# Linear attention with exponential features, then a gated causal layer: operand transposes of half the units by the DMA crossbar, feature weights by fp32 transfers, another order of products, and a new list

## The chip, the cores and the metric

The kernel runs on one core of a Trainium2 chip. The metric is the device time of one execution in microseconds (us), the median of several runs. A core has a tensor engine (PE; its weight loads are listed apart as PEld), a vector engine (DVE), a scalar engine (ACT), GpSimd (POOL) and a sync engine (SP). Each of them works through its own instructions in order, and semaphores make one wait for another. Products land in PSUM, which has 8 banks of 128 partitions by 512 fp32 numbers. Transfers run on 16 DMA engines. They are issued here from SP, ACT and POOL, and a transfer that changes the type is issued from POOL.

## The reference

For each of 8 batches and 8 heads, 576 tokens of 64 numbers are projected to 128 features, shifted by their largest magnitude, and taken through `exp` with both signs. The head outputs, side by side, then go through a gate and two matrix products.

```python
def phi(x):                                     # x: [8, 8, 576, 64], w_phi: [64, 128]
    proj = einsum('bhsd,df->bhsf', x, w_phi)
    proj = proj - max(abs(proj), axis=-1, keepdims=True)
    return concatenate([exp(proj), exp(-proj)], axis=-1)
q_p, k_p = phi(q), phi(k)
kv  = einsum('bhsf,bhsd->bhfd', k_p, v)
z   = sum(k_p, axis=2)
attn = einsum('bhsf,bhfd->bhsd', q_p, kv) / (einsum('bhsf,bhf->bhs', q_p, z)[..., None] + 1e-6)
x = attn.transpose(0, 2, 1, 3).reshape(8, 576, 512)
gate_pre[t] = sum over k of conv_w[k] * x[t + k - 4]       # causal, 5 taps
out = (sigmoid(gate_pre) * (x @ w_val)) @ w_out
```

## The kernel before

A *unit* is one pair of heads of one batch, its first 512 tokens: units 0 to 31, four to a batch. Units 32 to 39 are *tails*: the last 64 tokens of all heads of one batch. Each unit passes through small operations, and one string, `ORDER`, lists all of them by hand for the whole kernel, as `name.unit@banks:engine`. An engine's instructions stand in the order in which the list names them; semaphores are put in where one operation needs another. So the list alone sets what each engine, SP's and POOL's queues among them, does next, and a step that waits holds up all that stands behind it on its engine.

The operations of a unit, by their names in the list, with the line numbers of the old program:

- `LD` issues the loads of K, Q or V of a batch from POOL, fp32 in DRAM to bf16 in SBUF (L171, L177). Three batches of each have room.
- `T` transposes the unit's K and Q for the projection: eight 128x128 transposes on PE into one bank (L387). `C` copies the bank to SBUF, on DVE or ACT (L241, L239). The pool of these tiles `T` has room for five units.
- `PK`, `PA`, `PQ` are the projections by the feature weights `W2`: K with tokens on the partitions, Q likewise (for its largest magnitudes alone), and Q with features on the partitions (L437, L645). With `:W` they go over all 128 rows of the array with zero-padded weights (`W2Z`).
- `MA`, `MB`, `MQ` take the largest magnitudes on DVE (L503, L488). For units 0 and 1, and for tails, `MQ` writes `MQA`, and `SA`, which subtracts the maxima from `PQ`'s banks on PE, takes them straight from there (L661). For the others `MQ` writes `MQX`, `MT` transposes that on PE (L554), `MC` copies the result to `MQT`, and `SA` multiplies from `MQT`.
- `KA`, `KB` take the exponentials of K, one bank each, with both signs (L532). `XA`, `XB` take those of Q, one bank each, with both signs (L545): four instructions of 512 columns. Tails use `X0`, `X1`: one sign each, over both banks (L570).
- `E` and `V` scale V and its column of ones by the exponential of the maxima, mostly on POOL (L563, L609). `KV` sums K features times V over 16 matmuls of 65 columns and two of the tail (L622, L627); `KM` copies the result. `N` multiplies by the Q features, 16 matmuls of 65 columns (L699); `XN` divides on DVE (L717, L719). `XP` transposes the quotient into `XT`: by the DMA crossbar from SP for units 0 to 27 (L738), on PE for the last four and for tails, with `XX` copying the bank.

Per batch follow the gate (`GF`, `GT` on PE, `TH`, `HT` on ACT), the value product (`VA`, `VB`, L805), its product with the gate (`GV` on DVE, L821), the output product (`OA`, `OB`, L834), its copy (`OE`, on ACT L843 or DVE L845) and the stores from SP (`ST`, `SU`; at the end `SL`, half of whose transfers ACT issues). `HL` copies the first columns of `XT`, on POOL. `FL` multiplies zeros: matmuls that only keep PE running.

At the start, K of the first unit comes as fp32 by one transfer from SP and one from ACT, Q likewise behind it, and ACT and DVE cast them (`CK`, `CQ`). The feature weights come by one transfer from POOL that casts and repeats them, into `W2` (L195), from which `WB` fills `W2Z` on DVE.

## Time and profile before

| | |
|---|---|
| median of 3 runs | 231.88 us (231.78 to 236.46) |
| the profiled execution's own time | 231.9 us |
| its span (first to last instruction) | 230.1 us |
| mean granted TensorE clock | 0.985 of full speed |
| moved by DMA | 31.35 MB, mean 136 GB/s |

The page gives, for one profiled execution, each engine's busy time as a share of the span. A row of a group names line, engine, operation, `out<-in` with the shapes, the count, the busy time and the mean duration of one instruction, and the idle time just before them. Busy time is the union of the intervals, so that instructions that overlap count once. The chain that ended last is followed back from the last instruction: at each step to what released it, or to the instruction before it on its engine. A row of the timeline gives the start, the duration, the engine (ACTq and SPq are the queues that issue transfers) and what ran.

### The profile page before, as it was taken

The numbers are of one execution on the slowest core, as the hardware profiler recorded it, in microseconds if no ns is written. First come the engines' busy times: TensorE is split into PE (matmuls) and PEld (weight loads), VectorE is DVE, ScalarE is ACT, GpSimd is POOL, SyncE is SP. The second block draws the span as 40 slices with busy tenths as digits, with TensorE's granted clock in tenths as the row PEclk, the third lists the DMA queues.
The fourth block names the chain that finished last, engine by engine and source line by source line (L and its number), as shares of the span: only waits on it lengthen the run. The fifth ranks groups of instructions, "written<-read, shape, count | busy, mean of one in ns | idle before, by whom it ended". The sixth has DMA issues, their size and how long they took to land.

```text
span 230.1 us, 8985 instructions
## 1 busy us (share of the span) xinstructions
PE 204.2 (89%) x3834; PEld 140.6 (61%) x3862; DVE 190.2 (83%) x347; ACT 190.7 (83%) x419; POOL 130.9 (57%) x168
## 2 busy tenths in 40 slices
PE   0675989877989999999998999899999999999996
PEld 0363678556747576566756765668567666566642
DVE  6579999968889999879995999979998998757351
ACT  3189899996799999989998999899997989585530
POOL 8976668699299719393487343590299019500100
PEclk9999799999899999999999999999999999999999
DMA  6999974699969938899557796179940928403746
GB/s 123 190 203 219 262 131 51 99 239 126 150 91 198 191 78 117 132 191 193 87 71 129 99 161 179 50 105 145 227 117 6 140 46 187 115 3 95 177 140 187
DMA packets 42242, 31.35 MB, mean 136 GB/s; under 512 B 17877, under 2 KB 38229, under 8 KB 42202
## 3 DMA queue, kind: packets, MB, share of 16 engines
q0 software_dynamic: 21856, 14.93, 45.8%
q1 hardware_dynamic: 19802, 15.01, 30.7%
q10 hardware_dynamic: 544, 0.84, 1.2%
q8 instruction: 30, 0.49, 0.9%
q14 instruction: 10, 0.08, 0.1%
HBM read 32.58 MB, written 9.44 MB: 183 GB/s over the span
## 4 chain that ended last, share of the span: by engine, by line
PE 54%; ACT 27%; DVE 11%; issue 3%; DMA 3%; POOL 1%; DVEq 0%; ACTq 0%; POOLq 0%
ACT KT L532 10%; ACT QT L545 10%; PE PS L834 9%; PE PS L805 9%; PE PS L622 5%; PE PS L699 5%; PE PS L437 5%; DVE MQX L488 4%; PE PS L387 3%; PE PS L778 3%; PE PS L645 3%; DMA W<-in_w_phi_dram 3%; PE PS L661 2%; PE PS L282 2%; PE PS L885 2%
## 5 line engine op out<-in xcount | busy, mean ns | idle before, releaser
L609 POOL TENSOR_TENSOR VT<-vN,EA 128x1024 bf16<-128x1024 bf16 x30 | 57.2, 1905 | 43.1 <-ACT EA L563 30.1
L532 ACT ACTIVATE KT<-PS 128x512 bf16<-128x512 f32 x128 | 69.0, 660 | 8.3 <-DVE MKA L503 6.1
L545 ACT ACTIVATE QT<-PS 128x512 bf16<-128x512 f32 x128 | 68.8, 649 | 5.4 <-PE PS L661 5.2
L503 DVE TENSOR_REDUCE MKA<-PS 128x4 f32<-128x512 f32 x64 | 42.9, 682 | 2.4 <-PE PS L437 2.2
L488 DVE TENSOR_REDUCE MQX<-PS 128x8 bf16<-128x1024 f32 x30 | 36.6, 1219 | 3.4 <-PE PS L437 3.2
L805 PE MATMUL PS<-XT,WVAL 128*128 128x512 bf16 x128 | 35.4, 380 | 0.2
L834 PE MATMUL PS<-WOUT,GV 128*128 128x512 bf16 x108 | 31.3, 380 | 1.6 <-issue 1.1
L437 PE MATMUL PS<-W,T 64*128 64x128 bf16 x488 | 25.2, 226 | 2.8 <-ACT QT L545 0.8
L821 DVE SCALAR_TENSOR_TENSOR GV<-GATE,PS 128x512 bf16<-128x512 bf16 x32 | 21.4, 681 | 4.0 <-PE PS L805 3.8
L241 POOL COPY XT<-XT 128x1008 bf16<-128x1008 bf16 x8 | 8.2, 1031 | 27.8 <-DVE XT L241 19.8
L437 PEld LDWEIGHTS <-T 64*128 64x128 bf16 x488 | 16.7, 97 | 11.6 <-issue 7.1
L719 DVE TENSOR_TENSOR XN<-PS,RCPA 128x512 bf16<-128x512 f32 x32 | 22.1, 692 | 1.1
L622 PE MATMUL PS<-VT,KT 128*128 128x65 bf16 x512 | 22.1, 196 | 1.0 <-POOL VT L613 0.5
L241 DVE COPY T<-PS 128x1024 bf16<-128x1024 bf16 (+1 forms) x31 | 20.4, 666 | 2.3 <-PE PS L387 2.2
L699 PEld LDWEIGHTS <-QT 128*128 128x128 bf16 x512 | 19.6, 100 | 4.0 <-issue 0.6
L622 PEld LDWEIGHTS <-KT 128*128 128x128 bf16 x512 | 19.7, 99 | 3.7 <-issue 0.6
L699 PE MATMUL PS<-KVSA,QT 128*128 128x65 bf16 x512 | 21.4, 196 | 0.4 <-ACT KVSA L239 0.2
L600 POOL TENSOR_TENSOR VTZ<-vN,EA 64x512 bf16<-64x512 bf16 x16 | 16.7, 1042 | 8.7 <-ACT EA L563 8.2
L387 PE MATMUL PS<-ident_bf,kN 128*128 128x128 bf16 x128 | 13.6, 234 | 5.8 <-ACT kN L239 5.5
L794 ACT ACTIVATE GATE<-PS 128x1024 bf16<-128x1024 f32 x16 | 15.7, 1020 | 3.4 <-PE PS L778 3.4
L387 PE MATMUL PS<-ident_bf,qN 128*128 128x128 bf16 x128 | 13.7, 234 | 3.2 <-DVE qN L241 2.1
L834 PEld LDWEIGHTS <-GV 128*128 128x128 bf16 x128 | 10.4, 97 | 8.9 <-issue 1.2
(104 smaller groups left out, 367.6 us busy)
## 6 DMA issues: line engine op xcount, KB each, us to landing
out_dram<-OS SPq DMA_DIRECT2D x28, 256.0 KB, 3.9
kN<-in_k_dram POOLq DMA_DIRECT2D x14, 320.0 KB, 6.6
vN<-in_v_dram POOLq DMA_DIRECT2D x14, 320.0 KB, 7.2
qN<-in_q_dram POOLq DMA_DIRECT2D x7, 576.0 KB, 7.8
OS<-in_moe_w_val_dram SPq DMA_DIRECT2D x1, 1024.0 KB, 9.1
out_dram<-OSt SPq DMA_DIRECT2D x8, 128.0 KB, 2.4
vN<-in_v_dram POOLq DMA_DIRECT2D x4, 160.0 KB, 8.3
OS<-in_moe_w_out_dram SPq DMA_DIRECT2D x2, 256.0 KB, 6.7
```

The lines of the kernel that those rows point to most:

```text
L241: read(engines[eng].tensor_copy(dst, x), bank)
L387: nc.tensor.transpose(u.Tps[:, x, blk, :], a, ident_bf[:, :])
L437: nc.tensor.matmul(PS[:, bank[par], c0 + blk * P:c0 + (blk + 1) * P], u.T[r, i, blk, :], W2[r, :], start=True, stop=True,)
L488: read(nc.vector.tensor_reduce(MQX[:, i // G % NG, :].rearrange("p (r c) -> p r c", r=2)[:, :, c:c + 4], tokview(u.PA, 0, u, None), AX.X, ...
L503: read(nc.vector.tensor_reduce(out, half_ps(bank, x, out, wide), AX.X, ALU.max, apply_absolute_value=True,), [bank[x]])
L532: read(nc.scalar.activation(out, half_ps(u.PK, x, out, u.PKwide), AF.Exp, scale=1.0 if ft == 0 else -1.0,), [u.PK[x]])
L545: read(nc.scalar.activation(dst, PS[:, u.PQ[x], :].rearrange("p (x t) -> p x t", t=64), AF.Exp, scale=1.0 if ft == 0 else -1.0,), [u.PQ[x]])
L609: e.tensor_tensor(u.VT[:, :, :, 0:D], x.unsqueeze(1).to_broadcast([P, 2, n, D]), w.unsqueeze(3).to_broadcast([P, 2, n, D]), ALU.mult,)
L622: nc.tensor.matmul(PS[:, bank[0], c:c + E1], u.KT[:, ft, j // 2, j % 2, :], u.VT[:, ft, j, :], start=(ft == 0 and j == 0), stop=False, ski ...
L699: nc.tensor.matmul(PS[:, bank[c // 2], x * E1:(x + 1) * E1], u.QT[:, ft, c, h2, :, :].rearrange("p j t -> p (j t)"), kv[:, ft, h2, :], sta ...
L805: nc.tensor.matmul(PS[:, m.val[jt], :], WVAL[:, dt, jt * P:(jt + 1) * P], planes(xt(m.b), slice(0, P), dt, 4), start=(dt == 0), stop=(dt = ...
L834: nc.tensor.matmul(PS[:, bank, :], lhs(jt), WOUT[:, jt, :], start=(jt == 0), stop=(jt == 3))
```

## The change

1. K and Q of units 16 to 31 are no longer transposed by `T` and copied by `C`. Two transfers from SP for each unit, `TK` and `TQ`, write the tile `T` through the DMA crossbar. The function was in the program before, but the list didn't call it.
2. The feature weights come as fp32, by one transfer from SP and one from ACT between K and Q of the first unit. ACT casts them to `W2` (`W`), and DVE casts them to `W2Z` (`WB`). POOL's transfer is gone.
3. Units 2 to 7 take the way of units 0 and 1: `MQ` writes `MQA`, and `MT` and `MC` fall away (`MTF = 8`).
4. `KV` and `N` issue the same products in another order: four consecutive ones go to four places of the bank instead of adding to one place. `N` now has one start flag for each bank.
5. The list is new. Besides other banks and places, all units use `X0`, `X1` in place of `XA`, `XB`; the first K is cast by DVE; a clearing of `VTZ` (`VZ`), three of the four `DF` copies and three `HL` copies go from POOL to DVE; four units' `V` run on DVE instead of two; 16 projections have `:W` instead of 10; 7 `FL` stand within the kernel and 17 at its end, instead of 9 and 15.

```diff
+MTF = 8
 ORDER = """
-LD.1 CK.0:A LC.0 WB.0:D LD.0 CQ.0:D T.0@4 C.0:D LD.2 FL.6@6 LD.3 TX.0@0 CX.0:D PK.0@7,6 T.1@0 MA.0 C.1:D KA.0
+LD.1 CK.0:D W.0:A VZ.0:D T.0@1 C.0:D FL.16@0 FL.6@4 CQ.0:D WB.0:D PK.0@2,7 MA.0 TX.0@3 CX.0:D MB.0 LD.0 T.1@4
...
     main_dma((nc.sync, nc.scalar), "k", 0, 0, 1, first["k"])
+    W2 = const.tile([P, F], BF16, name="W2")
+    wtmp = const.tile([P, F], FP32, name="wtmp")
+    for t in range(2):
+        (nc.sync, nc.scalar)[t].dma_start(wtmp[t * 64:(t + 1) * 64, :], w_phi[:, :])
...
-    W2 = const.tile([P, F], BF16, name="W2")
-    nc.gpsimd.dma_start(W2[:, :], w_phi.unsqueeze(0).to_broadcast([2, D, F]))
...
+    def op_W(i, eng):
+        copy(eng, W2[:, :], wtmp[:, :])
+
     def op_WB(i, eng):
         for x in range(2):
             r = slice(x * 64, x * 64 + 64)
-            copy(eng, W2Z[r, x, :], W2[r, :])
+            copy(eng, W2Z[r, x, :], wtmp[r, :])
...
-        elif i < 2:
+        elif i < MTF:
             bankmax(MQA[:, i, :, :], u.PA, 0, u, u.PAwide)
...
     def op_KV(i, bank):
-        for ft in range(2):
-            for j in range(8):
-                c = (2 * ft + j // 4) * E1
+        for jj in range(4):
+            for x in range(4):
+                ft, j = x // 2, x % 2 * 4 + jj
+                c = x * E1
                 nc.tensor.matmul(
                     PS[:, bank[0], c:c + E1], u.KT[:, ft, j // 2, j % 2, :], u.VT[:, ft, j, :],
-                    start=(ft == 0 and j == 0), stop=False, skip_group_check=True,
+                    start=(jj == 0 and x == 0), stop=False, skip_group_check=True,
                 )
...
     def op_SA(i):
-                if u.tail or i < 2:
+                if u.tail or i < MTF:
...
     def op_N(i, bank):
-        for c in range(4):
-            for h2 in range(2):
-                x = (c % 2) * 2 + h2
-                for ft in range(2):
+        for half in range(2):
+            for ft in range(2):
+                for x in range(4):
+                    c, h2 = 2 * half + x // 2, x % 2
                     nc.tensor.matmul(
-                        PS[:, bank[c // 2], x * E1:(x + 1) * E1],
+                        PS[:, bank[half], x * E1:(x + 1) * E1],
                         u.QT[:, ft, c, h2, :, :].rearrange("p j t -> p (j t)"),
                         kv[:, ft, h2, :],
-                        start=(ft == 0), stop=(ft == 1),
+                        start=(ft == 0 and x == 0), stop=(ft == 1), skip_group_check=True,
                     )
```

The function behind `TK` and `TQ`, and that behind `X0` and `X1` (both unchanged):

```python
    def crossbar(i, x, name):
        u = units[i]
        if not hasattr(u, "T"):
            u.T = ktp.tile([P, 2, 4, P], BF16, name="T")
        j = 0 if name == "q" else 1
        nc.sync.dma_start_transpose(
            u.T[:, x, :, :], main[name, u.b][:, u.hp, j:j + 8, :].rearrange("p j d -> p (j d)"),
        )

    def qexp(u, ft):
        ...
        exps(u.QT[:, ft, :, :, :, :].rearrange("p c h r t -> p r (c h) t"), u.PQ, 4, ft)
```

Three places show how instructions move. A row gives the line, the operation and `out<-in` with the shape (x2: twice in a row); the new program's lines stand some six further down. The first is DVE behind the clearings that open the kernel. Before:

```order
L241 COPY W2Z<-W_111 64x128 x2
L241 CAST qN<-GV 128x576
L241 COPY T<-PS 128x512 x2
L503 TENSOR_REDUCE MKA<-PS 128x4
L241 COPY T<-PS 128x1024
```

Now:

```order
L243 CAST kN<-GV 128x640
L270 MEMSET VTZ_141 128x1040
L243 COPY T<-PS 128x512
L243 CAST qN<-GV 128x576
L243 CAST W2Z<-wtmp 64x128 x2
L508 TENSOR_REDUCE MKA<-PS 128x4
```

The cast of K and the clearing of `VTZ` have come to DVE, the copy of the first transposed K stands ahead of the cast of Q, and `W2Z`, on which nothing of the first unit rests now, stands behind both. The first maximum of K (`MKA`) stands right behind these.

The second place is SP, from the last crossbar transposes of batch 1 on. `XT<-XN` are the quotients (`XP`), `T<-qN` and `T<-kN` the new transfers, `out_dram` the stores. Before:

```order
L738 DMA_TRANSPOSE XT1_130<-XN_1269 128x4x128
L738 DMA_TRANSPOSE XT1_130<-XN_1369 128x4x128
L738 DMA_TRANSPOSE XT0_128<-XN_1804 128x4x128
L855 DMA out_0_dram<-OS_1722 64x1024 x2
L738 DMA_TRANSPOSE XT0_128<-XN_1888 128x4x128
L738 DMA_TRANSPOSE XT0_128<-XN_1946 128x4x128
```

Now:

```order
L744 DMA_TRANSPOSE XT1_132<-XN_1360 128x4x128
L402 DMA_TRANSPOSE T_1857<-qN_1415 128x4x128
L744 DMA_TRANSPOSE XT0_130<-XN_1869 128x4x128
L744 DMA_TRANSPOSE XT0_130<-XN_1826 128x4x128
L402 DMA_TRANSPOSE T_1968<-qN_1415 128x4x128
L744 DMA_TRANSPOSE XT0_130<-XN_1921 128x4x128
L744 DMA_TRANSPOSE XT0_130<-XN_1991 128x4x128
L402 DMA_TRANSPOSE T_1968<-kN_1425 128x4x128
L402 DMA_TRANSPOSE T_2275<-kN_1425 128x4x128
L402 DMA_TRANSPOSE T_1857<-kN_1425 128x4x128
L402 DMA_TRANSPOSE T_2275<-qN_1415 128x4x128
```

The transfers of K and Q of batch 4 (units 16 to 18 here) stand among and behind the four quotients of batch 2. SP has 60 crossbar transposes in all where it had 28.

The third place is ACT at the end of the kernel: `GATE` are the last gates, `OS` and `OSt` the copies of output products, the DMA rows the stores that ACT issues itself. Before:

```order
L794 ACTIVATE GATE0_5182<-PS_97 128x1024
L794 ACTIVATE GATE1_5203<-PS_97 128x1024
L843 ACTIVATE OSt_5221<-PS_97 128x512
L843 ACTIVATE OS_5232<-PS_97 128x512
L855 DMA out_0_dram<-OS_5232 64x512
```

Now:

```order
L800 ACTIVATE GATE0_4961<-PS_97 128x1024
L800 ACTIVATE GATE1_4975<-PS_97 128x1024
L900 ACTIVATE GATEt_5004<-PS_97 128x256
L849 ACTIVATE OS_5014<-PS_97 128x512
L861 DMA out_0_dram<-OS_5014 64x512
```

Before, one more copy and the other stores follow on ACT, while DVE copies two of the last four products; the tail's product `OSt` was copied ahead of them. Now the pair of copy and store stands four times on ACT, one behind the other, and the copy of the tail's product comes behind all of them as ACT's last instruction.

More of the change, by code (lines that the diff above doesn't have):

```diff
@@ L107 @@
+XX.39:D XX.28:A OE.27:A XP.31@5 OE.23:A ST.11 XX.31:D HL.7:D OB.26 OE.26:A VA.28@6 VA.30@7 GF.7@4,5,0,1 TH.14
+VA.31@3 VB.28 VA.29@2 GV.28 ST.13 VB.31 TH.15 VB.29 GV.29 VB.30 GV.31 GV.30 GT.7@4,5 HT.7 OA.30@0 OA.31@6
+OA.29@1 OB.30 OE.30:A OB.31 SL.30 OE.31:A SL.31 VT.7 GW.7 OB.29 OE.29:A SL.29 OA.28@0 OB.28 OT.3@6 OE.28:A
+SL.28 FL.15@2 FL.19@7 FL.20@0 FL.10@2 FL.11@5 FL.21@3 FL.4@2 FL.12@1 FL.5@7 FL.22@0 FL.23@0 FL.13@7 FL.8@5
+FL.0@0 FL.3@0 OF.3:A FL.14@0 SU.3 FL.2@0
 """
```

146 lines of the change are left out of this document (70 added, 76 removed).

## The prediction

> **What bounds the kernel now.** I read the page's busy times first, then the busy times in windows of 10 us, the chain that ended last with its shares and its pieces, and last the groups and the timeline where the change touches them. The page:
>
> ```profile
> span 230.1 us, 8985 instructions
> PE 204.2 (89%) x3834; PEld 140.6 (61%) x3862; DVE 190.2 (83%) x347; ACT 190.7 (83%) x419; POOL 130.9 (57%) x168
> ```
>
> Three engines stand within 6% of each other, so no single one bounds the whole. The windows say which does where (columns: stretch, its length, then each engine's busy time and count, granted PE clock, DMA share, GB/s):
>
> ```profile
> 20.00:30.00 10.00, 7.62 (x114) 5.11 (x113) 9.40 (x16) 8.91 (x22) 5.84 (x10) 0.83 1.26 247
> ...
> 110.00:120.00 10.00, 9.67 (x147) 6.31 (x143) 9.83 (x19) 10.00 (x25) 7.14 (x9) 1.00 0.46 65
> ...
> 180.00:190.00 10.00, 9.85 (x179) 6.94 (x180) 9.82 (x20) 9.41 (x24) 1.04 (x1) 1.00 0.55 92
> ```
>
> Where units 16 to 31 run, PE and DVE are at 97 to 99%, and ACT at 94 to 100%. POOL and the transfers have room. The chain, by share of the span, and in a second answer by share of the 94 us from 96 to 190 us alone, agrees:
>
> ```profile
> by line: ACT KT L532 10.2%; ACT QT L545 9.6%; PE PS L834 9.3%; PE PS L805 9.2%; PE PS L622 5.2%; PE PS L699 4.9%; PE PS L437 4.8%; DVE MQX L488 3.8%; PE PS L387 3.4%; PE PS L778 3.4%; issue 3.1%; PE PS L645 2.7%; DMA W<-in_w_phi_dram 2.5%;
> by line: ACT KT L532 13.5%; PE PS L805 9.5%; ACT QT L545 9.2%; PE PS L834 7.6%; PE PS L622 7.0%; PE PS L437 6.0%; PE PS L699 5.6%; PE PS L778 5.6%; PE PS L387 3.4%; PE PS L645 3.4%; DVE MQX L488 2.6%; issue 2.5%; PE PS L661 2.2%; ACT QTt L5
> ```
>
> It changes between PE and ACT all the time, with DVE in between. A cut on one engine alone would soon meet the next; this change takes work from all three.
>
> **Part 1: crossbar for K and Q of units 16 to 31.** What PE spends on these transposes, and DVE on their copies, over all 32 units:
>
> ```profile
> L387 PE MATMUL PS<-ident_bf,qN 128*128 128x128 bf16 x128 | 13.7, 234 | 3.2 <-DVE qN L241 2.1 <-issue 1.1
> L387 PE MATMUL PS<-ident_bf,kN 128*128 128x128 bf16 x128 | 13.6, 234 | 5.8 <-ACT kN L239 5.5 <-issue 0.2
> L241 DVE COPY T<-PS 128x1024 bf16<-128x1024 bf16 x29 | 19.6, 684 | 1.9 <-PE PS L387 1.9
> ```
>
> Half of 27.3 us of PE goes: 13.7 us. Of the copies, DVE loses 17 at 0.68 us, 11.5 us. On the chain they weigh less. From 96 to 190 us L387 has 3.4% of 94 us, 3.2 us. Three copies stand there as well, with other rows used below:
>
> ```profile
> 27.32 3.90 ACT QT L545 x8
> ...
> 112.50 0.92 ACT T L239
> ...
> 148.90 0.69 DVE T L241
> ...
> 161.65 0.92 ACT T L239
> ...
> 204.80 0.52 PE PS L622 x16
> 205.86 0.49 PE PS L699 x16
> ```
>
> They make 2.5 us, so 5.7 us of the chain go. I take that, since the chain shows what the end rests on; the bounds are 0 (the next engine is as late) and 13.7 us. What is late next is ACT, at 10.00 of 10 us in the window from 110 us.
>
> The new work lies on SP and the DMA engines: 32 transfers, each like a quotient's:
>
> ```profile
> L738 SPq DMA_TRANSPOSE XT<-XN x28: 1188/1197/2072, 34.7 to 189.1; - x28
> DMA to landing us min/median/max: 2.4/3.4/4.6
> q1 hardware_dynamic: 1632, 0.39, 19.3%
> ```
>
> Issuing takes 32 x 1.2 = 38 us of SP, which then has 60 x 1.2 = 72 us of transposes in 230. The last row is from 180 to 190 us, where four transposes alone ran on that queue: 19.3% of 10 us is 0.48 us of all 16 engines for each, 15 us for 32, or 7% of the span. I price both at nothing. The cover is the distance in the list: `TQ.17` and `TQ.16` stand some two units ahead of their projections, `TK.16` a whole gate ahead, and 3.4 us of landing fit into less than a unit (200 us / 32 = 6 us). Behind each on SP stand quotients and stores. A store can wait; a quotient held up holds the gate. If the cover fails, this is rival C.
>
> **Part 2: feature weights and opening.** The order of DVE and ACT at the start, before:
>
> ```profile
> 3.77 0.93 DVE L226 MEMSET VTZ<- 128x1040 bf16 x1 [0.17 <-issue]
> 4.69 0.27 DVE L230 MEMSET MQX<- 128x256 uint32 x1
> 7.32 0.58 DVE L241 COPY W2Z<-W 64x128 bf16<-64x128 bf16 x2 [2.36 <-DMA W<-in_w_phi_dram]
> 7.94 0.67 DVE L241 CAST qN<-GV 128x576 bf16<-128x576 f32 x1
> 8.53 0.41 DVE L241 COPY T<-PS 128x512 bf16<-128x512 bf16 x1
> 4.72 0.74 ACT L239 ACTIVATE kN<-GV 128x640 bf16<-128x640 f32 x1 [1.09 <-DMA GV<-in_k_dram]
> 10.57 2.06 ACT L532 ACTIVATE KT<-PS 128x512 bf16<-128x512 f32 x4 [5.11 <-DVE MKA L503]
> GV<-in_q_dram ACTq DMA_DIRECT2D x1, 144.0 KB, 4.2
> GV<-in_q_dram SPq DMA_DIRECT2D x1, 144.0 KB, 5.0
> ```
>
> DVE waits 2.36 us for the weights, and the first copy of `T` stands behind that wait. Now DVE, free at 4.96 us, casts K (0.74 us, ACT's price), clears `VTZ` (0.93), copies `T` (0.41, done at 7.05), casts Q (0.67) and `W2Z` (0.58). It reaches the first maximum at 8.3 us, and that takes 0.7 us: the first exponential at about 9.0 us instead of 10.57, so 1.5 us less. The weights take the place in the queues that Q had (4.2 to 5.0 us to landing, issued near 1.5 us), so they land by 6.5 us, ahead of the copy. Bounds: 0 if they come 1.5 us later, 2.5 us if POOL's earlier loads help as well (its weight transfer and its clearing are gone).
>
> **Part 3: exponentials of Q in two instead of four.** ACT's rows:
>
> ```profile
> L545 ACT ACTIVATE QT<-PS 128x512 bf16<-128x512 f32 x128 | 68.8, 649 | 5.4 <-PE PS L661 5.2
> L794 ACT ACTIVATE GATE<-PS 128x1024 bf16<-128x1024 f32 x16 | 15.7, 1020 | 3.4 <-PE PS L778 3.4
> 217.38 1.94 ACT L794 ACTIVATE GATE<-PS 128x1024 bf16<-128x1024 f32 x2 [0.85 <-PE PS L778]
> ```
>
> Back to back, 512 columns cost 3.90 / 8 = 0.49 us (row above) and 1024 columns 1.94 - 1.02 = 0.92 us. A unit gains 4 x 0.49 - 2 x 0.92 = 0.12 us, 32 units 3.8 us of ACT. On the chain L545 has 9.6% of 230 us, 22 us of 32 x 1.96 = 63 us, a third; so I take 1.2 us, with bounds of 0 and 6.1 us (by the busy shares, 68.8 / 128 = 0.54 and 15.7 / 16 = 0.98 us). The Trainium skill, page "ScalarE: Activation LUTs", section "What ACT_TABLE_LOAD costs", gives an ACTIVATE 186 ns and 0.833 ns per column, of which 93 ns overlap with the next: by that the pair of 512 and 1024 columns would be 0.52 and 0.95 us, 6.0 us over all units, and this term 2.0 us instead of 1.2. The trace's 0.49 us is nearer to the columns alone than the page has it.
>
> **Part 4: order of products.** `KV` ran 16 products in 0.52 us, `N` the same size in 0.49, where only pairs add to one place. If four places make `KV` as quick, its chain share (5.2% of 230 = 12 us) falls by 6%, 0.7 us. Bounds 0 and 2 us. `N` gains nothing.
>
> **Part 5: units 2 to 7 without `MT` and `MC`, more wide projections, moves to DVE.** Priced at nothing: in the first third ACT hides what PE and DVE do more, since PE had 2.4 us of 10 free in the window from 20 us. Two more `V` on DVE cost about the 3.9 us that its copies leave four times over. Bounds 1 us of gain (a shorter way from maximum to exponential) and 2.5 us of loss.
>
> **Part 6: the end.** ACT's last rows, and the chain's:
>
> ```profile
> 223.43 0.51 ACTq L855 DMA_DIRECT2D out_dram<-OS  x1
> 223.99 0.60 ACT L843 ACTIVATE OS<-PS 128x512 f32<-128x512 f32 x1 [0.59 <-PE PS L834]
> 224.61 2.03 ACTq L855 DMA_DIRECT2D out_dram<-OS  x3
> ...
> 220.61 4.26 PE PS L834 x19
> ```
>
> Four pairs of copy (0.60) and issue (0.51), and then the tail's copy, make 5.0 us on ACT, from the first product's end on. Before, DVE had two of the copies, and ACT two copies and four issues. PE has 12 output products behind the first (4.26 / 19 = 0.22 us each) and a tail's value product, some 3 us. So the end lies about 1 us further behind the last product than before; bounds 0 and 1.5 us. The 17 `FL` behind it cost nothing beside the stores' landing.
>
> **Sum.** -1.5 (opening) - 5.7 (crossbar) - 1.2 (exponentials) - 0.7 (products) + 0 + 1.0 (end) = -8.1 us: a span of 222.0 us. The profiled execution took 231.9 us with a span of 230.1, so 1.8 us lie around it, and it equals the median of 231.88. That gives 223.8 us.
>
> **The rivals.**
>
> A, *all three engines get lighter and the chain shortens with them*: PE's busy time falls by its full 13.7 us and nothing else comes late. Then the sum is -16.1, and the time 215.8 us. For it speaks that PE and DVE are both near 10 of 10 in the window from 180 us; against it that ACT loses only some 4 of 190.7 us.
>
> B, *ACT is the bound*, as in the window from 110 us. PE's and DVE's relief turns into idle time. What is left is the opening (1.5), the exponentials' full 3.8 us at most, and 1.8 us of ACT's copies of `T`, less 1.0 at the end: at most 6.1 us, and 3.5 us with the chain's share of the exponentials. The time is 226 to 228.4 us, within 2%. Against it: PE has the larger share of the chain.
>
> C, *SP's order holds the projections up*, the case on the slower side. A `TK` waits for K's load and for a free `T` tile, and all behind it waits too, quotients included. Were each of 16 units to wait 0.5 us, the 8.1 us would be gone; from 0.8 us each (8.1 + 4.6 = 12.7 us) it is slower by 2%. With the slowest landing, 4.6 us, instead of 3.4, a unit whose transfer is just in time loses 1.2 us, and the time is 223.8 + 19.2 = 243 us. Against it: the transfers stand a unit or more ahead.
>
> D, *PE pauses long enough to be clocked down*. In the window from 20 us PE was busy for 7.62 of 10 us and had 0.83 of its clock; at 9.67 it had all. If the missing transposes open such pauses in three windows, PE loses 17% of 10 us in each, 5 us: 228.8 us. The Trainium skill, page "TensorE: Matmul & The Clock Gate", section "Part 1: The HAM clock gate (the "warmup" mystery)", says that the clock halves after an idle window of some 3.4 us; the row at 0.83 fits that in kind, but no row after 110 us does.
>
> E, *the order of products does nothing*: 224.5 us, inside the forecast.
>
> **How the numbers follow.** The forecast, with E in it (221 to 226 us), gets 0.53, A (215 to 221) 0.22, B (226 to 229) 0.14, D 0.04 and C 0.07. About 2% is what a measurement of this kernel tells from no change: 227.2 and 236.5 us. Faster takes the forecast, A and 0.04 of B: 0.79. Within 2% lie the rest of B, D and a mild C: 0.16. Slower is the rest of C: 0.05. The range goes from A's 215.8 to B's 228.8 us and leaves out the best of A and C, some 0.15.
>
> **What would show it.** In the changed profile the first `KT` exponential should start near 9.0 us; L387 should have half its count; a pair of `QT` rows should show 0.92 us to the next; `KV` should show 0.49 us for 16; PE should never wait for `T<-kN` or `T<-qN`; ACT's busy share should rise. A wait of `PK` or `PQ` for a DMA row of 0.5 us or more in each unit, or ACT at 95% and more, would make the prediction wrong.

## The result, and the profile after

The changed kernel took 244.29 us (median of 4 runs, 242.92 to 246.21), where the kernel before took 231.78, 231.88, 236.46 and 238.62 us in the same comparison (median 234.17). Some executions of a kernel are 1.5% or more slower than its fastest, and the medians here and below take them in while the ratios leave them out, so the ratio is the one to go by where the two differ. The ratio is 1.054, with a 95% interval of 1.042 to 1.067: slower by 5% or 12.5 us, where 223.8 us and a range of 215.8 to 228.8 us were forecast. The profiled execution took 246.21 us, its span is 244.4 us, and the mean granted clock of PE fell from 0.985 to 0.951.

The page of the changed kernel gives the busy times and the chain by engine:

```profile
span 244.4 us, 8652 instructions
PE 205.2 (84%) x3693; PEld 137.1 (56%) x3720; DVE 192.5 (79%) x340; ACT 186.6 (76%) x353; POOL 122.5 (50%) x155
PE 36%; DVE 26%; ACT 16%; DMA 15%; issue 3%; POOL 2%; ACTq 1%; DVEq 0%; SPq 0%; POOLq 0%
```

The three engines have about the busy time that they had before, in a span that is 14.3 us longer. So none of them became the bound; they wait together. The chain shows for what: transfers have 15% of it, some 37 us (before, they had 3%). PE's busy time should have fallen by a dozen us, and it rose by one. The groups show a part of the reason (count, then busy us and mean ns):

```profile
L392 PE MATMUL PS<-ident_bf,kN 128*128 128x128 bf16 x64 | 7.5, 247 | 7.2 <-DVE kN L243 5.4 <-issue 1.3 <-ACT QTt L575 0.3
L392 PE MATMUL PS<-ident_bf,qN 128*128 128x128 bf16 x64 | 7.4, 248 | 1.0 <-DVE qN L243 1.0
...
L811 PE MATMUL PS<-XT,WVAL 128*128 128x512 bf16 x128 | 34.8, 397 | 0.0
```

The transposes are down to 14.9 us from 27.3. But the same 128 value products, which had 380 ns each, now have 397. Over the whole kernel the mean clock, 0.951 instead of 0.985, stretches 205 us of work on PE by some 7 us (an estimate from these numbers); the rest of the dozen isn't accounted for. The windows (columns as before the change: PE, PEld, DVE, ACT, POOL, clock, DMA share, GB/s) show where PE slowed down:

```profile
40.00:50.00 10.00, 6.05 (x76) 4.23 (x71) 9.10 (x15) 5.94 (x10) 9.65 (x12) 0.71 0.41 79
70.00:80.00 10.00, 6.62 (x151) 4.54 (x145) 4.99 (x9) 4.79 (x9) 5.38 (x8) 0.75 0.99 136
110.00:120.00 10.00, 9.46 (x187) 6.93 (x190) 9.42 (x19) 10.00 (x20) 1.88 (x3) 1.00 1.23 161
140.00:150.00 10.00, 6.29 (x85) 3.62 (x88) 5.44 (x11) 6.67 (x15) 0.00 (x0) 0.83 1.26 195
```

The stretch from 110 us is nearly as tight as before on PE, DVE and ACT. In each of the other three PE stands still for over 3 us in one piece (3.07, 3.38 and 3.13 us in the timeline), and these windows have a clock of 0.71, 0.75 and 0.83. The chain's pieces of transfer (start, us, what) name what each pause goes back to:

```profile
2.44 5.65 DMA GV<-in_q_dram
27.33 10.88 DMA OS<-in_moe_w_val_dram
67.77 8.58 DMA XT<-XN
135.62 11.71 DMA T<-qN
```

Besides a wait for Q in the opening these are the load of the value weights, a transpose of quotients, and one of the new transposes of Q. The first pause is a wait for DVE, which itself stood behind POOL and the weights. For the crossbar transfers PE waited directly (us in total, times, longest):

```profile
PE PS L880 <- DMA XT<-XN: 5.5, 3, 3.4
PE PS L442 <- DMA T<-qN: 3.1, 1, 3.1
```

In the profile before, PE waited for no transfer at all. The rows of the crossbar transposes (min/median/max of the issue on SP in ns, then of the time to landing in us) say that the last two are outliers by far. The quotients':

```profile
L744 SPq DMA_TRANSPOSE XT<-XN x28: 1189/1257/2449, 34.9 to 203.7; - x28
DMA to landing us min/median/max: 2.4/3.6/8.6
```

Those of K and Q:

```profile
L402 SPq DMA_TRANSPOSE T<-qN x16: 1188/1340/2524, 86.2 to 188.4; - x16
L402 SPq DMA_TRANSPOSE T<-kN x16: 1189/1258/2633, 99.3 to 184.6; - x16
...
DMA to landing us min/median/max: 2.4/4.7/11.7
```

In the profile before, no transpose landed later than 4.6 us. The largest piece of transfer in the chain of the changed kernel is one that a projection of Q waits for, and with it all that stands behind on PE:

```profile
134.95 0.33 PE PS L442 x8
135.28 0.24 PE PS L667 x8
135.51 0.04 SPq L402
135.55 0.07 issue
135.62 11.71 DMA T<-qN
147.32 0.05 issue
147.37 0.61 PE PS L442 x8
```

Between 135.5 and 147.3 us nothing on the chain computes. PE does, with products that stood ahead in its order, until 144.2 us; it is idle for the last 3.13 us alone. So a piece of 11.7 us on the chain doesn't mean 11.7 us of idle engines. The start of `GATEt`, one per batch, places the losses in time (us, from the timelines; `e4_earlyval` is told of below):

| | 1 | 2 | 3 | 4 | 5 | 6 | 7 | 8 | end of span |
|---|---|---|---|---|---|---|---|---|---|
| before | 46.4 | 71.0 | 98.6 | 123.0 | 146.4 | 171.5 | 193.7 | 216.1 | 230.1 |
| after | 51.9 | 77.8 | 106.4 | 131.0 | 160.9 | 182.8 | 214.7 | 233.4 | 244.4 |
| e4_earlyval | 48.4 | 72.7 | 101.5 | 126.3 | 154.8 | 177.3 | 207.9 | 226.6 | 237.7 |

The lists place a gate differently within its batch, so a single column can mislead by some us. The trend doesn't: 5.5 us are lost by the first gate, 8.0 by the fourth and 14.5 by the fifth, and from there to the end, where 14.3 us are lost, nothing is lost or won, although the second half is where the transposes were taken off PE.

### The profile page after: what moved, and what is told of

The parts are those of the page before. It is cut to its first block, busy times and chain, and to the rows that moved or that the text cites. A ratio compares the mean times of both kernels' runs of the same rounds, so it can differ in the third digit from the quotient of the medians.

```text
span 244.4 us, 8652 instructions
## 1 busy us (share of the span) xinstructions
PE 205.2 (84%) x3693; PEld 137.1 (56%) x3720; DVE 192.5 (79%) x340; ACT 186.6 (76%) x353; POOL 122.5 (50%) x155
## 4 chain that ended last, share of the span: by engine, by line
PE 36%; DVE 26%; ACT 16%; DMA 15%; issue 3%; POOL 2%; ACTq 1%; DVEq 0%; SPq 0%; POOLq 0%
PE PS L811 7%; PE PS L840 6%; ACT QT L575 6%; ACT KT L537 5%; DVE MKA L508 5%; DMA T<-qN 5%; DMA OS<-in_moe_w_val_dram 4%; DVE MQX L493 4%; DMA XT<-XN 4%; PE PS L442 3%; PE PS L784 3%; DVE XN L725 3%; PE PS L705 3%; PE PS L628 2%; DMA GV<-in_q_dram 2%
## 5 line engine op out<-in xcount | busy, mean ns | idle before, releaser
L614 POOL TENSOR_TENSOR VT<-vN,EA 128x1024 bf16<-128x1024 bf16 x28 | 54.5, 1947 | 33.5 <-ACT EA L568 27.3
L575 ACT ACTIVATE QT<-PS 128x1024 bf16<-128x1024 f32 x64 | 62.7, 1047 | 5.6 <-PE PS L667 5.3
L811 PE MATMUL PS<-XT,WVAL 128*128 128x512 bf16 x128 | 34.8, 397 | 0.0
L493 DVE TENSOR_REDUCE MQX<-PS 128x8 bf16<-128x1024 f32 x24 | 29.3, 1220 | 6.7 <-PE PS L442 6.0
L840 PE MATMUL PS<-WOUT,GV 128*128 128x512 bf16 x108 | 32.1, 386 | 1.1 <-issue 0.5
L628 PE MATMUL PS<-VT,KT 128*128 128x65 bf16 x512 | 21.1, 195 | 0.9 <-DVE VT L618 0.5
L243 POOL COPY XT<-XT 128x1008 bf16<-128x1008 bf16 x5 | 5.1, 1024 | 25.7 <-DMA XT<-XN 9.7
L811 PEld LDWEIGHTS <-WVAL 128*128 128x128 bf16 x128 | 11.1, 102 | 10.9 <-issue 2.1
L849 ACT ACTIVATE OS<-PS 128x512 f32<-128x512 f32 x19 | 11.4, 612 | 7.6 <-PE PS L840 5.8
L477 DVE TENSOR_REDUCE MQA<-PS 128x8 bf16<-128x1024 f32 (+1 forms) x16 | 15.1, 950 | 0.5 <-PE PS L442 0.5
## 6 DMA issues: line engine op xcount, KB each, us to landing
OS<-in_moe_w_val_dram SPq DMA_DIRECT2D x1, 1024.0 KB, 10.9
```

Of the source, the lines that this page charges most:

```text
L493: read(nc.vector.tensor_reduce(MQX[:, i // G % NG, :].rearrange("p (r c) -> p r c", r=2)[:, :, c:c + 4], tokview(u.PA, 0, u, None), AX.X, ...
L575: read(nc.scalar.activation(dst, banks(*bank)[:, :, 0:n * P].rearrange("p r (x t) -> p r x t", t=dst.shape[-1]), AF.Exp, scale=1.0 if ft = ...
L614: e.tensor_tensor(u.VT[:, :, :, 0:D], x.unsqueeze(1).to_broadcast([P, 2, n, D]), w.unsqueeze(3).to_broadcast([P, 2, n, D]), ALU.mult,)
L628: nc.tensor.matmul(PS[:, bank[0], c:c + E1], u.KT[:, ft, j // 2, j % 2, :], u.VT[:, ft, j, :], start=(jj == 0 and x == 0), stop=False, ski ...
L811: nc.tensor.matmul(PS[:, m.val[jt], :], WVAL[:, dt, jt * P:(jt + 1) * P], planes(xt(m.b), slice(0, P), dt, 4), start=(dt == 0), stop=(dt = ...
L840: nc.tensor.matmul(PS[:, bank, :], lhs(jt), WOUT[:, jt, :], start=(jt == 0), stop=(jt == 3))
```

## The experiments

Three theories were tried. V: the load of the value weights starts too late. L: a crossbar transpose that flies beside other transfers lands late, and what reads it waits. S: SP issues in order and takes long for a transpose, so that the quotients' transposes start late. The rival to all of them: the terms of the sum, not the waits, were wrong. Times are medians; a ratio is that to the kernel before in the same comparison, with its 95% interval.

| run | us | ratio |
|---|---|---|
| e3_crossbar | 251.56 | 1.078 (1.068 to 1.088) |
| e5_nocross | 256.85 | 1.108 (1.096 to 1.120) |
| e4_earlyval | 239.49 | 1.030 (1.022 to 1.038) |
| e6_ahead | 239.46 | 1.032 (1.021 to 1.043) |
| e24_gaps | 237.42 | 1.020 (1.012 to 1.028) |
| e13_xpe | 249.54 | 1.067 (1.056 to 1.078) |
| e7_vpool | 243.63 | 1.046 (1.036 to 1.056) |
| e14_fourexp | 241.21 | 1.031 (1.022 to 1.041) |
| e10_dummy | 247.52 | 1.064 (1.055 to 1.073) |
| e11_plain | 237.31 | 1.006 (0.998 to 1.013) |
| e20_spread | 237.94 | 1.023 (1.014 to 1.032) |
| e21_const | 248.42 | 1.071 (1.063 to 1.079) |
| e26_rest | 235.06 | 1.013 (1.007 to 1.018) |
| e27_wide15 | 236.12 | 1.013 (1.008 to 1.018) |
| e1_products | 233.07 | 0.996 (0.993 to 1.000) |
| e2_twoexp | 272.70 | 1.171 (1.161 to 1.180) |

### The value weights

In the old list, `Z.0:P` (which opens the staging tile) and `LW.0` (the load) come early. In the new one, `Z.0` is on DVE, behind the maxima and copies of the first units. The timelines show the shift (start, us, engine, line). SP before:

```profile
18.21 0.42 SPq L332 DMA_DIRECT2D OS<-in_moe_w_val_dram  x1
```

DVE and then SP after:

```profile
27.21 1.22 DVE L477 TENSOR_REDUCE MQA<-PS 128x8 bf16<-128x1024 f32 x1
27.23 0.06 DVE L333 MEMSET OS<- 128x1 f32 x1
...
27.33 0.42 SPq L337 DMA_DIRECT2D OS<-in_moe_w_val_dram  x1
```

A clearing of 0.06 us, put into DVE's order, delays a load of 10.9 us by 9.1 us. (The list of moves from POOL to DVE further up leaves `Z.0` out.) Behind the load stand POOL's rounding (`CV`), `DG`, `DF` and then the first gate. The experiment moves two entries of the new list:

```diff
-... T.33@6,7 C.33:D Z.0:D LW.0 E.2 X0.1 ...
+... T.2@5 C.2:A C.3:D Z.0:D LW.0 MQ.1 ...
+... T.33@6,7 C.33:D E.2 X0.1 ...
```

> The changed kernel, with the clearing of the staging tile (Z.0) and the load of the value weights behind it (LW.0) moved ahead in the list, behind the copy C.3, so that DVE reaches it near 16 us instead of 27 us. Theory (the weights' late landing at 38 us holds POOL's casts, the gate's weights and so the first gate up): 4 to 5 us faster than the changed kernel, 239 to 241 us, first gate near 50 us. Rival (something else is as late there): within 1 us of the changed kernel's 244 us.

It came out at 239.49 us, and the first gate at 48.4 us instead of 51.9. Its interval ends at 1.038, where the changed kernel's begins at 1.042, so theory V is shown: by the medians it has 4.8 of the 12.5 us that were lost. All that follows on the new list starts from this kernel.

### The crossbar transposes alone, in the old list

The kernel before, with the transposes of K and Q of units 16 to 31 by the crossbar and nothing else of the change:

```diff
-T.16@4 ... C.16:D ... T.19@6 ... C.19:D          (and so on to unit 31)
+T.14@4 TK.16 TQ.16 ... TK.19 TQ.19               (issued where the list had T of the unit ahead)
```

> The kernel before, with nothing changed but that K and Q of units 16 to 31 come by crossbar transposes from SP, each pair issued where the list had the T of the unit ahead of it. Theory 1 (crossbar transfers that land late, beside loads and stores, hold projections up): slower than before, 235 to 240 us, with PE waiting for T<-qN or T<-kN rows for 3 us and more in all. Theory 2 (the crossbar saves PE and DVE work, as predicted, and the loss of the changed kernel lies in its list): 224 to 229 us, no such waits.

251.56 us is above what either theory gave. So this part, which made up 5.7 of the forecast's 8.1 us of gain, costs 18.6 us in the old list. The other way round, the changed kernel with `T` and `C` put back into the new list by a simple rule:

```diff
-TQ.16 ... TK.16
+T.16@5 ... C.16:D                                (for each of units 16 to 31)
```

> The changed kernel, with the crossbar transposes of units 16 to 31 undone: T on PE into a bank that is free at that place, some twenty entries of the list ahead of the projection, and C on DVE (ACT for units 20 and 26). Theory 1: the wait of 11.7 us for T<-qN near 136 us goes, 236 to 240 us. Theory 2: the list is as bad and PE and DVE have 13.7 and 10 us more to do: 246 to 252 us.

It is slower still (256.85 us). The rule only looked for a free bank, and the places that it found were not chosen with the rest of the list, so this run doesn't price the crossbar by itself. The next four do: they keep `T` and `C`, and add the 32 transfers into tiles that nothing reads.

```diff
+        spare[n] = ktp.tile([P, 4, P], BF16, name="SPARE")
         nc.sync.dma_start_transpose(
-            u.T[:, x, :, :], main[name, u.b][:, u.hp, j:j + 8, :].rearrange("p j d -> p (j d)"),
+            spare[n][:, :, :], main[name, u.b][:, u.hp, j:j + 8, :].rearrange("p j d -> p (j d)"),
         )
```

> The kernel before with its own transposes and copies left where they are, and beside them the 32 crossbar transposes of K and Q of units 16 to 31, issued on SP at the same places as in e3_crossbar but into spare tiles that nothing reads. TensorE and VectorE have no less to do, and no projection waits for a crossbar landing: what the run loses is what the traffic alone costs. Theory (the crossbar traffic delays other transfers, above all the transposes of the quotients): 8 to 18 us slower than before, so 241 to 251 us, with transposes of the quotients that land in 7 us or more on the chain. Rival (what cost e3 was the projections' waiting for K and Q): within 2 us of before, 231 to 235 us.

```diff
-        nc.sync.dma_start_transpose(
-            spare[n][:, :, :], main[name, u.b]...
+        nc.sync.dma_start(
+            spare[n][:, :, :].rearrange("p c t -> p (c t)"), main[name, u.b]...
```

> As e10_dummy, but each of the 32 extra transfers is a plain copy of the same 128 x 512 bfloat16 elements between the same tiles instead of a transpose. If bytes and SP's issues cost the time, it is as slow as e10_dummy within 2 us. If transposing costs it, this run is within 2 us of before while e10_dummy is not.

The transposes cost 14.5 us although nobody waits for them. The same bytes as plain copies cost nothing that the ratio can tell. Their ten runs spread from 232.34 to 241.59 us, so a small cost isn't ruled out, but every run with transposes took 245 us or more. One place where that happens stands in the chain of e10_dummy (start, us, what):

```profile
124.86 1.30 SPq L399
126.22 1.26 SPq L399
127.59 2.53 DMA XT<-XN
130.16 0.40 PE PS L876 x5
```

SP issues two of the extra transposes, 1.3 us each, and only then the quotients' transpose for which the gate waits. That one lands in 2.53 us, as fast as any. So the next pair tells the place in SP's order from the rest. One has the transposes in four groups in the gaps between the quotients', from a constant tile; the other has the same constant tile at e10_dummy's places.

```diff
-... T.14@4 TK.16 TQ.16 N.10@2,3 ...
+... XP.11 (nine entries) TK.16 TQ.16 (seven entries) TK.17 TQ.17 ...
-            spare[n][:, :, :], main[name, u.b]...
+            spare[n][:, :, :], zero[:, :],
```

> As e10_dummy with the same 32 extra transposes, but all from one constant tile (no load is waited for) and issued in four groups of eight that start ten entries of the list after the last quotients' transpose of a batch, where SP is idle for some 12 us in e10_dummy's trace, so that none stands ahead of a quotients' transpose. Theory S (what costs e10_dummy its 14.5 us is SP's order: each issue takes 1.2 to 2.4 us, and the quotients' transposes are issued behind them): within 3 us of before, 230 to 236 us. Theory L (it is the traffic, which makes landings late wherever it is issued): 241 us or more.

> e10_dummy with its 32 extra transposes at the same places of the list, but from the constant tile that e20_spread used. Theory S (place: the quotients' transposes are issued behind them on SP): as slow as e10_dummy, 244 to 249 us. Rival (source: reading K and Q on SP holds back something, or SP waits there for a load): as e20_spread, 236 to 240 us.

Only the place differs between the two, and it is worth 10.5 us: 248.42 against 237.94, with intervals far apart. What it changes is seen where PE waits for the quotients (us, times; e21_const, then e20_spread):

```profile
  PE PS L876: 10.7, 6
  PE PS L876: 1.2, 1
```

The quotients' transposes themselves land alike in both (2.4/3.8/7.1 us in e21_const, 2.4/3.7/7.0 in e20_spread). So they aren't later from issue to landing; they are issued later. That the extra transposes land late in the gaps doesn't matter, as e20_spread's row shows:

```profile
DMA to landing us min/median/max: 2.5/6.0/11.8
```

They land later than those of e21_const (2.4/4.1/7.7) and cost a third as much, since no quotient stands right behind them on SP. Where the 2.3% that are left come from, these runs don't tell.

### The landing by itself

A kernel that does nothing but transfers, one phase after the other:

```python
# transposes beside casting loads
phase((LDK, LDV, LDK2, LDV2))            # waits for all that went before
both(nc.gpsimd, 3, LDK, LDV)             # 320 KB each, fp32 to bf16
both(nc.gpsimd, 7, LDK2, LDV2)
for x in range(8):
    nc.sync.dma_start_transpose(DST[:, x, :].rearrange("p (c t) -> p c t", t=P), SRC[:, x, :])
```

> None of the reference is computed; zeros are stored. One phase after the other, with nothing else running: 8 transposes of 128 x 512 by SP alone, 8 copies of the same bytes alone, 4 casting loads of 320 KB by POOL alone, 4 plain loads of the same fp32 bytes by ACT's queue alone, then transposes and copies beside each kind of load, 8 transposes issued by two queues in turn, and 4 transposes of twice the size. Theory (a transpose that shares the DMA engines with a casting load lands late): 2.4 to 4 us from issue to landing alone, 7 us or more beside casting loads; beside plain loads between these. Rival (what is late in the kernels is SP's order, not the landing): under 5 us in all phases. An issue on SP is expected to take 1.2 us for a transpose and 0.5 to 0.6 us for a copy, as in e10_dummy and e11_plain.

> As e12_micro (nothing of the reference is computed), with 8 casting loads of 320 KB in each of those phases, issued as the transposes begin, so that they last as long. Theory L: transposes beside them land in 6 us or more in the median, against 2.5 us alone; copies beside them in less than 5 us. Rival S: under 4.5 us at most, as in e12_micro.

In the first version the loads were nearly over when the transposes began: 2.5 us in the median and 4.4 at most, which looked like theory S. The second corrects it. Its rows are those of transposes alone, copies alone, transposes beside casting loads, and copies beside casting loads (issue on SP in ns, then landing in us):

```profile
L88 SPq DMA_TRANSPOSE DST<-SRC x8: 1244/1267/1315, 21.1 to 30.3; - x8
DMA to landing us min/median/max: 2.5/2.5/2.5
...
L92 SPq DMA_DIRECT2D DST<-SRC x8: 538/599/600, 35.3 to 39.7; - x8
DMA to landing us min/median/max: 2.0/2.1/2.1
...
L105 SPq DMA_TRANSPOSE DST<-SRC x8: 1190/1312/3409, 77.6 to 90.1; - x8
DMA to landing us min/median/max: 6.5/10.0/12.7
...
L111 SPq DMA_DIRECT2D DST<-SRC x8: 464/673/784, 103.0 to 108.0; - x8
DMA to landing us min/median/max: 2.1/7.1/7.5
```

Beside casting loads a transpose lands in 10.0 us, four times as late as alone, and a copy in 7.1. The expectation had copies under 5 us, so it isn't the transposing alone that makes a landing late: any transfer that shares the engines with the loads is late. By these medians the transpose is some 3 us later than the copy. What is particular to the transpose is its issue: 1.27 us of SP against 0.60. The Trainium skill, page "Advanced Engine Details and Errata", section "X-Bar Transpose (TRN2)", has transposes as fast as regular transfers. For the landing alone that nearly holds (2.5 against 2.1 us); for SP's time and for the landing beside loads, these rows say otherwise. The Trainium skill, page "DMA: Bandwidth & Descriptors", section "SWDGE vs HWDGE vs iDMA", says that casting loads and transposes feed different queues of the same engines, which go round between them. The rows agree with that: neither stops, and both are late. The last two casting loads landed after 16.9 us in the median beside the transposes, and after 11.8 us alone.

### The crossbar transposes in the new list

Three kernels on e4_earlyval. The first puts each `TK` and `TQ` some 50 entries ahead of its projection, and the second into the gaps between the quotients' transposes:

```diff
-    ktp = pool("ktp", 5)
+    ktp = pool("ktp", 7)
-... VB.5 GV.5 TK.16 GT.2@2,3 ... PK.16@2,3
+... XP.11 KA.15 MB.15 OB.2 TK.16 OT.0@6 ... GT.2@2,3 ... PK.16@2,3
```

> e4_earlyval (239.5 us) with every TK and TQ put at least some 50 entries of the list ahead of its projection (they stood 3 to 10 entries ahead for units 16, 17, 19, 20 and 29) and two more buffers for T. Theory (a landing of up to 11.7 us against a lead of some 3 us is what PE waits for): 233 to 236 us, no wait of PE for T left on the chain. Rival (the traffic delays the quotients whenever it is issued, so the lead buys nothing): 238 to 241 us, with the wait for XT in place of that for T.

```diff
-... TQ.17 (395) XP.8 (401) ... TQ.16 (424) XP.10 (426) ... TK.16 (475) ... PK.16 (484)
+... TQ.16 (345) TK.16 (357) TQ.17 (369) TK.17 (380) ... XP.8 (404) ... PK.16 (489)
```

(The numbers are places in the list.)

> e4_earlyval (239.5 us) with the transposes of K and Q moved to the stretches of the list between the last quotients' transpose of one batch and the first of the next, all of them earlier than they stood or at most some ten entries later, and 7 buffers of T in place of 5. Theory S (SP's order): the quotients' and the projections' waits for the crossbar go, 233 to 236 us. Rival L (a landing beside casting loads is late wherever it is issued): 238 us or more, with waits for XT or T of 6 us or more left on the chain, as in e6_ahead.

A longer lead bought nothing: 239.46 us. In e6_ahead's chain no wait for `T` is left, and the quotients' transposes take over:

```profile
64.87 8.41 DMA XT<-XN
94.53 7.28 DMA XT<-XN
124.36 2.44 DMA XT<-XN
147.17 6.62 DMA XT<-XN
173.61 2.43 DMA XT<-XN
```

So the short lead, which I had suspected after the first reading, was not the cause, and the rival holds. The gaps gave 2 us more, 237.42 us, but the intervals of the three overlap, so that isn't shown. The first of these waits is no matter of K and Q at all: at 64.87 us none of their transposes has been issued. In the changed kernel the same one, issued at 67.77 us, flies beside the casting loads that POOL issued from 67 us on; in the kernel before, the last transpose of that batch was issued at 64.84 us, 0.4 us ahead of the loads at 65.23 us, and none landed later than 4.6 us. A shift of about a us between the two queues goes with the difference; it wasn't tried alone. Such a landing needs none of the new transposes and not the new list. The profiled execution of e1_products (236.39 us; the old list with another order of products, told of below) has it too, and PE waited 3.2 us for it:

```profile
63.84 9.17 DMA XT<-XN
```

The third takes the quotients off the crossbar:

```diff
-XP.9 ... 
+XP.9@5 ... XX.9:D        (on PE, with a copy, for units 0 to 27)
```

> e4_earlyval (239.5 us) with the quotients of units 0 to 27 transposed on TensorE into a free bank of PSUM and copied out by ScalarE and VectorE in turn, as the list does already for units 28 to 31; the crossbar has K and Q of units 16 to 31 alone. PE gets 28 x 0.22 = 6.2 us, ScalarE and VectorE 14 copies of some 0.5 us each. Theory (the quotients' late landings are most of the loss: 6% of the chain, 14 us, in e4_earlyval's profile): 229 to 234 us, though PE has more to do. Rival (the waits for K and Q grow in their place, or PE's work fills what is saved): 238 us or more.

249.54 us, 10 us slower: the rival. What the waits for `XT` have on the chain wasn't to be had by giving the work to PE and the copies to ACT and DVE.

### The small terms

The four units' `V` back on POOL, and the exponentials of Q in four instructions again, both on e4_earlyval:

```diff
-V.1:D ... V.22:D ... V.26:D ... V.29:D
+V.1:P ... V.22:P ... V.26:P ... V.29:P
```

> e4_earlyval (239.5 us) with the rounding of V of units 1, 22, 26 and 29 back on POOL (after put it on VectorE, where it took 0.21 to 1.90 us). Theory (a VectorE copy that runs beside POOL's is stretched to POOL's end): 0.5 to 3 us faster, 236.5 to 239 us. Rival (POOL hands V over later and its products wait): 239.5 to 241 us.

```diff
-X0.0 X1.0 ...
+XA.0 XB.0 ...            (units 0 to 31)
```

> e4_earlyval (239.5 us) with the exponentials of Q of units 0 to 31 again as four of 512 columns, at the places of the two of 1024: 64 more ScalarE instructions, QT back to 68.8 us from 62.7. Theory (ScalarE is on a fifth of the chain or less, so a part of the 6.1 us counts; the prediction took 1.2 us): 240 to 242 us. Rival (all of it counts): 245 to 246 us. If it is not slower at all, the wider exponentials bought nothing here.

e7_vpool missed its expectation: it is 4 us slower in the median, though the intervals still overlap. So no loss by the move to DVE is seen, even if small copies there ran long (below). e14_fourexp differs from its base by 0.1% in the ratio, where each interval reaches about 1% to both sides: if the wider exponentials bought anything in the new list, it was too little to be seen.

Then the parts in the old list, each without the others but for e26_rest, which joins the opening, the products and 15 units' wider exponentials:

```diff
-... XA.2 MA.3 E.2 XB.2 ...
+... X0.2 X1.2 MA.3 E.2 ...             (e2: units 0 to 31; e26, e27: the 15 whose banks are adjacent)
-CK.0:A LC.0 WB.0:D LD.0 CQ.0:D
+CK.0:A W.0:A LC.0 LD.0 CQ.0:D WB.0:D   (e26)
```

> The kernel before, with nothing changed but that the exponentials of Q of units 0 to 31 are two instructions of 1024 columns instead of four of 512, at the place of the first of them. As the prediction had it: 1.2 us less, 230.7 us (bounds 0 and 3.8 us less). Rival (both banks are held until both signs are done, and waits eat the gain): 232 to 234 us.

> The kernel before with the parts of the change that need neither its crossbar transposes nor its list: feature weights by fp32 transfers and the copy W, the products of KV and N in the new order, and the exponentials of Q of 1024 columns for the 15 of the first 32 units whose two banks are adjacent in the list of before. By the prediction's own terms: opening 0.9 us (as the changed kernel's first exponential shows), products up to 0.7 us, exponentials some 15/32 of 1.2 us or more: 229.5 to 231.5 us where before is 233. If the terms of the sum were worth nothing here: 232.5 us or more.

> The kernel before with the exponentials of Q of 1024 columns for the 15 units whose banks are adjacent, both at the place where the first half stood. By the prediction's term (1.2 us for 32 units, up to 6.1): 0.6 to 2.9 us faster, 230.5 to 233 us. Rival (the first now waits for both banks' products and both banks come free later, which TensorE pays): 234.5 us or more.

> The kernel before with the products of KV and N in the new order alone, nothing else moved. By the prediction's term: 0.7 us faster (0 to 2), so 231.5 to 233.5 us where before is 233.5. Rival (the order of products is what made e26_rest slower): 234.5 us or more.

The order of products is the one part whose time came out where its forecast had it: 0.4% faster, 0.9 us, though the interval (0.0 to 0.7%) ends at no gain at all. Its chain has pieces like these (`KV`, then `N`):

```profile
130.38 0.49 PE PS L623 x16
142.11 0.51 PE PS L700 x16
```

`KV` went from 0.52 to 0.49 us, as forecast, and `N`, which was to gain nothing, from 0.49 to 0.50 or 0.51. The wider exponentials cost 3.1 us for 15 units, and 40 us where all 32 have them, many over banks that aren't adjacent. An instruction is as short as forecast; e27_wide15's chain has pairs like this:

```profile
99.87 1.84 ACT QT L568 x2
```

That is 0.92 us each, and ACT's busy time fell by 1.4 us against before. But the two stand where the list had the first of the old pairs, wait for both banks, and give both back at the end. Which of these makes the loss wasn't tried apart. e26_rest is slower by as much as e27_wide15 alone, so its ratio shows nothing of its opening and products. Since e1_products is the only kernel with a ratio below 1, and its interval reaches 1, no version was found that clearly beats the kernel before.

## Why the prediction was wrong

**Part 1 failed, at the sentence "I price both at nothing".** The cover named was the distance in the list: "`TQ.17` and `TQ.16` stand some two units ahead of their projections, `TK.16` a whole gate ahead". Counted in the new list, a unit is some 29 entries, and `TK.16`, `TK.17`, `TK.19`, `TQ.20` and `TQ.29` stand 3 to 10 entries ahead of the projection. But e6_ahead shows that this slip wasn't what mattered. The step that failed is the landing of 3.4 us, taken from transposes that in the old list never landed later than 4.6 us, as if it went with the instruction. Beside casting loads it is 10.0 us (e25_micro8), and the 11.7 us on the changed kernel's chain began 1.2 us after four such loads had been issued. PE, which was never to wait for `T`, waited 3.1 us for Q, and 5.5 us for quotients, where it had waited for no transfer before. SP's 38 us failed too: that quotients stand behind them was named and priced at nothing, and in the old list that place alone is worth 10.5 us. In the new list another place gained nothing that is clear of the spread (e24_gaps). The gain side wasn't reached: after the fifth gate, with the transposes off PE, the changed kernel runs no faster than before. Two readings beside the sum were off as well: the list takes 16 copies from DVE (30 to 14) and not 17, and the 97 to 99% of PE and DVE hold for the two windows that were shown; in the windows between 100 and 190 us DVE had 75 to 99%.

**Rival C was the case, with a chance of 0.07 against it.** Its price, 243 us, is close to the 244.3 us measured, but by luck, since the way there was another: not 1.2 us in each unit, but a few landings of 8 to 12 us on the chain, each with some 3 us in which PE stood still, and the late load of the value weights, which rival C doesn't have. "The transfers stand a unit or more ahead" was the reason for the low chance, and it was an average over the list.

**Part 5, "moves to DVE" at nothing, failed.** The bound was 2.5 us of loss, for DVE's time. The cost came through a row of 0.06 us, `Z.0`, which the prediction didn't look at: 4.8 us, since a load waited for it.

**Part 2 was mis-sized.** The first exponential came at 9.7 us, not 9.0: Q's transfer, moved behind the weights, landed after 5.65 us, and DVE waited for it. 0.9 us of 1.5 were won there, and lost again before the first gate.

**Part 3 had the right price and the wrong place.** 0.92 us an instruction was right. That a shorter instruction shortens the chain was not shown: nothing to be seen in the new list, 3.1 us of loss in the old.

**Part 4 was right in its mechanism**: sixteen products of `KV` take 0.49 us. Its size, 0.7 us, fits the 0.9 us measured alone, but that measurement doesn't exclude nothing; and `N` lost 0.01 to 0.02 us each, which the part had at nothing.

**Part 6 was too small.** ACT's copies and issues at the end follow each other every 1.18 us, from 235.17 to 239.88 us:

```profile
235.17 0.60 ACT L849 ACTIVATE OS<-PS 128x512 f32<-128x512 f32 x1 [1.39 <-PE PS L840]
...
239.88 0.60 ACT L849 ACTIVATE OSt<-PS 128x512 f32<-128x512 f32 x1 [0.58 <-ACT OS L849]
```

That makes 5.3 us where 5.0 were forecast. From the last `GV` to the end there are 10.1 us, and before there were 8.1: 2 us lost instead of 1.

**Rival D's mechanism came, for another reason.** The clock fell to 0.71, 0.75 and 0.83 in three windows, not because transposes were missing but because PE waited for a transfer, or for DVE that waited for one. With it the same products took 397 ns instead of 380, and a part of the 12.4 us that PE was relieved of went.

Open is what the new list is worth without its waits. In e4_earlyval PE waited 8.5 us for crossbar transfers, and the kernel is 3% (7 us) slower than before; that the one makes the other fits in size, but none of the three changes meant to take these waits away brought the time back. Some 2% remain in e24_gaps, and neither that they are landings nor that they are the list's order was shown.

## What to carry to other kernels

Before work is moved from an engine to the transfers, look at what else flies at that moment: price the landing from a row that had the same neighbours, and count what stands behind the issue on its queue. A list by hand hides its own timing: the same edit in e20_spread and e21_const differs by 10.5 us by place alone, and an entry of 0.06 us that opens a tile can hold back a load of 10.9 us. A chain's share of waiting is no offer either: a piece of 11.7 us left PE idle for 3.1 us, in e6_ahead one wait gave way to another, and in e13_xpe to more work.

## What the runs showed of the hardware

- A transpose of 128 x 512 bf16 takes SP 1.27 us to issue, and a copy of the same bytes 0.60. Four transposes of twice the size took 1.32 us each and landed in 3.3 us (e25_micro8): the issue hardly grows with the size.
- Beside casting loads, a transpose of 2.5 us landed in 6.5 to 12.7 us; beside plain loads of the same fp32 bytes, in 2.8 to 12.8 us with a median of 5.9. Copies fared little better (7.1 and 5.4 us in the median).
- A small conversion on DVE took up to nine times its shortest time. In the changed kernel the one of 128 x 16 behind `V` took (ns, POOL's ahead of DVE's):

```profile
L618 POOL CAST VT<-EA x28: 244/253/1245, 20.3 to 215.9; 128x16 bf16<-128x16 f32 x28
L618 DVE CAST VT<-EA x4: 211/1075/1903, 23.2 to 212.1; 128x16 bf16<-128x16 f32 x4
```

- Both that took 1.90 us ran beside a product on POOL and ended within 0.1 us of its end; that one waits for the other is a reading of this, and wasn't tried alone.
